# Cutting the last weight transfer of a decode kernel in two: the second half of the last wo block arrives as two transfers of one row each per partition

## The chip, the cores and the metric

The kernel runs on one core of one Trainium2 chip. The metric is device time in microseconds (us). "Before" is the kernel as it was, "the change" the kernel with the diff below.

The engines have their names from the profile: PE is the matrix engine (TensorE), DVE the vector engine, ACT the scalar engine, and SP (SyncE) here issues transfers and waits. A DMA transfer copies between the chip's main memory and its on-chip buffer. A semaphore is a counter on which an engine can wait; a transfer has "landed" when its semaphore has had all of its updates. The "chain of waits" is what the profile shows when it is followed back from the last instruction, at each step to what released it.

The unchanged kernel took 1344.42 us (median of 3 runs, 1344.25 to 1344.47). Its span in the profile, from the first to the last instruction, is 1342.8 us.

## The reference, cut to what matters

```python
# 4 sequences, one token each, model width 1024, 32 heads of 128, 8192 cached keys
q = (x @ wq) ...                                  # 4 x 32 heads x 128
p = softmax(q . k_cache * 128**-0.5)
o = p . v_cache
a = o.reshape(4, 32 * 128) @ wo                   # wo: 4096 x 1024, bf16, 8 MB
b = x + sigmoid(x . w_r) * ((silu(x @ w_gate) * (x @ w_up)) @ w_down)
out = sigmoid(x . gate_w) * a + (1 - sigmoid(x . gate_w)) * b     # 4 x 1 x 1024
```

The caches are 537 MB (512 MiB) of bf16 and the weights nearly all the rest of 576 MB. Every byte is read once, so the kernel is a long stream of loads. The product with wo comes last, because it needs the finished attention output.

## The kernel before

SP issues all loads in program order. wo is handled in 8 blocks, numbered 0 to 7. A block holds 512 rows of wo: four consecutive rows of 1024 elements for each of 128 partitions. One row is 2 KB of one partition, so a block is 8 KB per partition and 1 MB in all.

```python
FR = 4                      # rows of wo per partition and block
NB, NH = 512, 2             # a row is multiplied in two halves of 512 columns
wov = A_wo.rearrange("(g p r) n -> p g r n", p=P, r=FR)

def mm_acc(out_ap, lhsT, rhs, start=False):
    nc.tensor.matmul(out_ap, lhsT=lhsT, rhs=rhs, start=start, stop=True, skip_group_check=True)

def wo_block(g, r0=0, r1=FR):
    home, at = divmod(g, 4)
    # ... (a slot of the ring buffer holds four blocks)
    w = wo_home[home][:, at]
    nc.sync.dma_start(out=w[:, r0:r1].rearrange("p r n -> p (r n)"),
                      in_=wov[:, g, r0:r1].rearrange("p r n -> p (r n)"))
    def use():
        for r in range(r0, r1):
            for n in range(NH):
                mm_acc(acc[:, n * NB:(n + 1) * NB], LT[:, r, g, :], w[:, r, n * NB:(n + 1) * NB])
    return use

# ... the end of the kernel, NWB = 8:
last = [wo_block(g) for g in range(2, NWB - 2)]
last += [wo_block(g, r, r + FR // 2) for g in (NWB - 2, NWB - 1) for r in (0, FR // 2)]
last.pop(0)()
# ... (last of the attention output, flushed between the first blocks)
last.pop(0)()
o_rows(GE, NWB)
for use in last:
    use()
res = turned(Bn, D)
nc.vector.tensor_copy(out=res[:, 0:NB], in_=acc[:, 0:NB])
nc.sync.dma_start(out=out2[:, 0:NB], in_=res[:, 0:NB])
nc.scalar.copy(out=res[:, NB:D], in_=acc[:, NB:D])
nc.scalar.dma_start(out=out2[:, NB:D], in_=res[:, NB:D])
```

So blocks 2 to 5 come as one transfer of 1024 KB each, and blocks 6 and 7 as two of 512 KB each (two rows per partition). The wait for a transfer stands before the first matmul that reads it. DVE copies the first 512 output columns and ACT the second.

## Time and profile before

| | before |
|---|---|
| time, median of 3 runs | 1344.42 us |
| span in the profile | 1342.8 us |
| bytes moved, mean rate | 576.18 MB, 429 GB/s |
| PE / DVE busy | 77% / 46% |

The first extract is from the profile's page of the kernel before. The span is cut in 40 equal slices; each digit is the busy share of one slice in tenths, and the last row gives the rate in GB/s.

```profile
span 1342.8 us, 7621 instructions
PE   2665877787788687778987779598778679877897
DVE  2555655544346554335455546146555244556000
DMA  9999999999999999999999999999999999999997
GB/s 414 434 434 430 432 436 430 444 433 418 445 430 424 440 431 425 437 436 432 432 438 431 426 433 430 434 436 435 432 423 441 430 427 431 436 426 443 423 423 331
```

The DMA engines are busy from the first slice to the last, and only the last slice falls off. The kernel is bound by its stream. What is left to win is in the last slice, where the stream ends and something must still be done with what came last.

The second extract is the timeline of the last 6 us of the same kernel: start, duration, engine, line and operation; in brackets the idle time ahead of the instruction and what ended it. Weight loads (PEld) are left out.

```profile
1336.09 1.34 PE L279 MATMUL acc<-ring,LT 128*4 128x512 bf16 x5
...
1337.66 1.02 PE L279 MATMUL acc<-ring,LT 128*4 128x512 bf16 x4 [0.23 <-DMA ring<-in_A_wo_dram]
...
1338.89 1.02 PE L279 MATMUL acc<-ring,LT 128*4 128x512 bf16 x4 [0.21 <-DMA ring<-in_A_wo_dram]
...
1339.74 0.68 DVE L588 CAST TB<-acc 4x512 bf16<-4x512 f32 x1 [8.29 <-PE acc L279]
1339.95 0.57 ACT L590 CAST TB<-acc 4x512 bf16<-4x512 f32 x1 [13.55 <-PE acc L279]
1340.44 0.29 SPq L589 DMA_DIRECT2D out_dram<-TB  x1
1340.56 0.55 ACTq L591 DMA_DIRECT2D out_dram<-TB  x1
```

The third extract is the chain of waits that ended last, of the same kernel from 1325 us on: start, duration, what.

```profile
1323.81 15.04 DMA ring<-in_A_wo_dram
1338.85 0.04 issue
1338.89 1.04 PE acc L279 x4
1339.93 0.02 issue
1339.95 0.57 ACT TB L590
```

Read together: the last 512 KB land at 1338.85 us. Only then can four matmuls run, which end at 1339.93. ACT's copy follows, then the output transfer. PE waited 0.23 us and 0.21 us for the two last transfers.

Matmuls here start 0.216 us apart, and the last one takes 0.38 us to its modelled end. Four take 3 x 0.216 + 0.38 = 1.03 us.

The trace also records every DMA packet and every semaphore update. A transfer is shared among 16 engines, and each engine reports its own share, so the landing of a transfer has 16 times. For the last transfer of the kernel before they are these (us):

```
1332.23 1332.49 1332.68 1333.25 | 1336.70 1336.78 1336.83 1336.84 1337.03 1337.04 1337.18 1337.30 | 1338.23 1338.26 1338.66 1338.85
```

Four engines are done about 6 us before the last four. The transfer has landed when the slowest has its share. The last four 512 KB transfers landed at 1335.11, 1336.37, 1337.62 and 1338.85, one per 1.24 us. That is the slowest engine working off 8 packets of 4 KB at a time: the trace does not number the engines, but the packets that end with the last one can be followed back from 1338.27 us to 1332.20, each starting about 155 ns after the one before.

### The profile page before, as it was taken

How to read it: one execution, taken by the hardware profiler on the slowest of the kernel's cores; microseconds unless marked ns; L12 is line 12 of the kernel's file. 1: busy time of each engine (PE TensorE's matmuls, PEld its weight loads, DVE VectorE, ACT ScalarE, POOL GpSimd, SP SyncE). 2: the span in 40 equal slices, each digit the busy share in tenths (PEclk: the TensorE clock that was granted, in tenths of full speed). 3: DMA queues.
4: the chain of work that ended last, by engine and by line, in shares of the span. 5: the costliest groups of instructions: out<-in, count | busy, mean ns of one | idle time of the engine just before them, and what ended most of it. 6: DMA issues, size and time to landing. Idle time of an engine off the chain costs nothing.

```text
span 1342.8 us, 7621 instructions
## 1 busy us (share of the span) xinstructions
PE 1033.8 (77%) x4536; PEld 226.1 (17%) x2348; DVE 612.4 (46%) x358; ACT 50.6 (4%) x46; POOL 55.3 (4%) x90
## 2 busy tenths in 40 slices
PE   2665877787788687778987779598778679877897
PEld 0111111111111111111211112111111112111221
DVE  2555655544346554335455546146555244556000
ACT  0000100001000010001000010000100010000100
POOL 2000010001000010001000010000100010000100
PEclk9687988988999898889888889898889799889799
DMA  9999999999999999999999999999999999999997
GB/s 414 434 434 430 432 436 430 444 433 418 445 430 424 440 431 425 437 436 432 432 438 431 426 433 430 434 436 435 432 423 441 430 427 431 436 426 443 423 423 331
DMA packets 14172, 576.18 MB, mean 429 GB/s; under 512 B 1582, under 2 KB 1590, under 8 KB 2108
## 3 DMA queue, kind: packets, MB, share of 16 engines
q1 hardware_dynamic: 14132, 575.69, 99.5%
q8 instruction: 27, 0.44, 0.1%
q14 instruction: 5, 0.04, 0.0%
q10 hardware_dynamic: 8, 0.00, 0.0%
HBM read 575.68 MB, written 0.01 MB: 429 GB/s over the span
## 4 chain that ended last, share of the span: by engine, by line
DMA 65%; DVE 20%; PE 12%; another core or an unknown queue 1%; ACT 0%; issue 0%; SPq 0%; DVEq 0%
DMA ring<-in_A_k_cache_dram 56%; DVE TB L443 20%; PE o_ps L523 10%; DMA ring<-in_A_v_cache_dram 7%; DMA x<-in_gate_w_dram 2%; DMA ring<-in_A_wo_dram 1%; PE S_ps L449 1%; ACT PB L494 0%; PE S_ps L313 0%; PE acc L313 0%; PE small L543 0%; ACT OS L535 0%; PE acc L279 0%; DVE OS L536 0%
## 5 line engine op out<-in xcount | busy, mean ns | idle before, releaser
L443 DVE STREAM_TRANSPOSE TB<-ring 128x2048 uint32<-128x2048 uint32 x256 | 567.3, 2278 | 495.2 <-DMA ring<-in_A_k_cache_dram 493.9
L449 PE MATMUL S_ps<-TB,Z 128*128 128x512 bf16 x2048 | 520.0, 409 | 218.7 <-DVE TB L443 218.5
L523 PE MATMUL o_ps<-ring,PB 128*32 128x512 bf16 x2048 | 461.9, 389 | 52.5 <-DMA ring<-in_A_v_cache_dram 47.9
L449 PEld LDWEIGHTS <-Z 128*128 128x128 bf16 x1024 | 105.5, 103 | 628.8 <-issue 627.3
L523 PEld LDWEIGHTS <-PB 128*32 128x32 bf16 x1024 | 100.9, 99 | 410.0 <-issue 401.3
L536 DVE SCALAR_TENSOR_TENSOR OS<-o_ps,mE,OS 128x512 f32<-128x512 f32 x8 | 6.0, 751 | 104.1 <-ACT OS L535 104.1
L474 ACT ACTIVATE PTs<-S_ps,negm 128x1024 bf16<-128x1024 f32 x8 | 8.9, 1114 | 1024.9 <-DVE negm L471 1024.9
L425 POOL TENSOR_TENSOR Z<-qa,mq 128x16 bf16<-128x16 bf16 x32 | 9.1, 286 | 744.4 <-PE S_ps L449 654.7
L496 POOL COPY PB<-PT 32x1024 bf16<-32x1024 bf16 x16 | 30.4, 1903 | 82.1 <-PE o_ps L523 81.7
L494 ACT COPY PB<-PT 32x1024 bf16<-32x1024 bf16 x16 | 30.5, 1907 | 1.5 <-DVE PT L476 1.3
L376 DVE CAST LT<-small 128x64 bf16<-128x64 f32 x2 | 0.5, 225 | 40.6 <-PE small L374 40.6
L226 PE MATMUL small<-identb,x 6*128 6x6 bf16 x8 | 0.6, 197 | 22.6 <-DMA x<-in_gate_w_dram 22.6
L467 POOL PARTITION_ALL_REDUCE gmx<-mex x8 | 3.2, 396 | 340.7 <-DVE mex L464 340.7
L462 DVE TENSOR_REDUCE m<-S_ps 128x1 f32<-128x1024 f32 x8 | 9.8, 1225 | 15.9 <-PE S_ps L449 15.9
L279 PE MATMUL acc<-ring,LT 128*4 128x512 bf16 x64 | 15.0, 378 | 2.0 <-DMA ring<-in_A_wo_dram 1.4
L476 DVE STREAM_TRANSPOSE PT<-PTs 128x1024 bf16<-128x1024 bf16 x8 | 10.0, 1245 | 10.2 <-ACT PTs L474 10.2
L279 PE MATMUL acc<-ring,hT 128*4 128x512 bf16 x56 | 12.2, 379 | 0.0
L535 ACT ACTIVATE OS<-o_ps,mE 128x512 f32<-128x512 f32 x8 | 5.5, 687 | 158.8 <-PE o_ps L523 158.8
L313 PE MATMUL o_ps<-ring,xw 128*4 128x512 bf16 x56 | 6.0, 555 | 5.0 <-DMA ring<-in_B_w_gate_dram 5.0
L543 PEld LDWEIGHTS small<-selg,OS 128*128 128x128 f32 x64 | 9.0, 208 | 4.1 <-issue 3.9
L543 PE MATMUL small<-selg,OS 128*128 128x16 f32 x64 | 8.7, 269 | 0.0
L548 DVE SCALAR_TENSOR_TENSOR OT<-small,sgb,rinv 128x16 bf16<-128x16 f32 x8 | 1.8, 225 | 10.5 <-PE small L543 10.5
(71 smaller groups left out, 67.1 us busy)
## 6 DMA issues: line engine op xcount, KB each, us to landing
ring<-in_A_k_cache_dram SPq DMA_DIRECT2D x14, 4096.0 KB
ring<-in_A_v_cache_dram SPq DMA_DIRECT2D x14, 4096.0 KB, 31.2
ring<-in_B_w_gate_dram SPq DMA_DIRECT2D x1, 7168.0 KB, 37.6
ring<-in_B_w_up_dram SPq DMA_DIRECT2D x1, 7168.0 KB, 39.2
ring<-in_B_w_down_dram SPq DMA_DIRECT2D x2, 3584.0 KB, 27.5
ring<-in_A_wo_dram SPq DMA_DIRECT2D x6, 1024.0 KB, 21.0
ring<-in_A_v_cache_dram SPq DMA_DIRECT2D x2, 2048.0 KB, 26.8
ring<-in_A_v_cache_dram SPq DMA_DIRECT2D x4, 1024.0 KB, 25.0
```

What stands on the lines that cost most here:

```text
L279: nc.tensor.matmul(out_ap, lhsT=lhsT, rhs=rhs, start=start, stop=True, skip_group_check=True)
L313: nc.tensor.matmul(ps[32 * k:32 * k + Bn, z, :], lhsT=xT[TW * half + t], rhs=cols(w, t, 4 * z + k), start=(half + t == 0), stop=(half == 1 ...
L425: nc.gpsimd.tensor_tensor(out=Z[:, :, QP - 1:QP - 1 + P].rearrange("p e (q c) -> p e q c", c=QP)[:, :, :, 0], in0=qa[:, :, h0:h0 + NQ, b], ...
L443: nc.vector.transpose(out=flat_t.bitcast(U32), in_=kn[:, c * CJ * Dh:(c + 1) * CJ * Dh].bitcast(U32))
L449: nc.tensor.matmul(sps[:, z, :], lhsT=Z[:, he, s:s + P], rhs=T[:, 16 * z:16 * z + 16, half, :, e], start=(t == 0 and n == 0 and he == 0), ...
L462: nc.vector.tensor_reduce(out=m1[:], in_=sps[:].rearrange("p z n -> p (z n)"), axis=AX.X, op=ALU.max)
L474: nc.scalar.activation(out=PTs[:], in_=sps[:].rearrange("p z n -> p (z n)"), func=ACT.Exp, bias=negm[:, 0:1], scale=scale, accum_out=rs[:, ...
L476: nc.vector.transpose(out=PT[:].rearrange("p j i -> p (j i)"), in_=PTs[:])
L494: nc.scalar.copy(out=Bv[at, :, :, q, :], in_=Pv[at])
L496: nc.gpsimd.tensor_copy(out=Bv[at, :, :, q, :], in_=Pv[at])
L523: nc.tensor.matmul(o_ps[row:row + NM, e, :], lhsT=PB[:, RD * t + c, z, w].rearrange("p e s j -> p (e s j)"), rhs=vn[:, j0 * Dh:(j0 + 4) * ...
L543: nc.tensor.matmul(oT[:, :], lhsT=o_sb[:, q * Dh:(q + 1) * Dh], rhs=selg[:, q].rearrange("p t s -> p (t s)"), start=(q == 0), stop=(q == 3))
```

## The change

The intent: of the last 512 KB, the first row per partition can be multiplied while the second is still coming. So two matmuls instead of four are left when the last byte is there.

```diff
     last = [wo_block(g) for g in range(2, NWB - 2)]
-    last += [wo_block(g, r, r + FR // 2) for g in (NWB - 2, NWB - 1) for r in (0, FR // 2)]
+    cuts = [(NWB - 2, 0, 2), (NWB - 2, 2, 4), (NWB - 1, 0, 2), (NWB - 1, 2, 3), (NWB - 1, 3, 4)]
+    last += [wo_block(*cut) for cut in cuts]
     last.pop(0)()
```

Transfers, matmuls and their order stay otherwise as they were. SP issues one transfer more (two of 256 KB in place of one of 512 KB), and PE has one wait more, before the last two matmuls.

## The prediction

> **What bounds the kernel now.** The memory stream. The page of the kernel before shows a span of 1342.8 us, 429 GB/s on average and a DMA row at 9 tenths in 39 of 40 slices; PE is 77% busy, DVE 46%. The change touches only the last 5 us. There the chain of waits reads: landing of the last wo transfer until 1338.85 us, four matmuls 1338.89 to 1339.93 (1.04 us), the ACT copy at 1339.95 (0.57 us), then the output transfer. The timeline shows PE waiting 0.23 and 0.21 us for wo transfers before its last two groups of four matmuls.
>
> The packet records show what paces the end. The fastest engine's share of the last 512 KB transfer lands at 1332.23 us, the slowest's at 1338.85. On the slowest, the last four 512 KB transfers complete at 1335.11, 1336.37, 1337.62 and 1338.85, one per 1.24 us: 8 packets of 4 KB, 159 ns each. The last landing is that engine's backlog; the same bytes cannot land earlier.
>
> **What the change does.**
> - Bytes, matmuls and their order stay. The instruction order shows one more issue on SP and one more wait on PE, before the last two matmuls.
> - Removed from the chain: the two matmuls of row 2. Row 2 lands at about 1338.25 us, and its matmuls run while row 3 still comes. After the last landing two matmuls remain: one pitch of 0.216 us plus one duration of 0.38 us, 0.60 us instead of 1.04. Gain: 0.43 us.
> - Added: 2 KB packets in place of 4 KB ones. Packets of 16, 8 and 4 KB took 613, 313 and 159 ns, the few of 2 KB 84 ns; 16 x 84 instead of 8 x 159 ns would be 0.07 us on the slowest engine, rather less as starts are 155 ns apart. One semaphore packet (9 ns) comes on top. The Trainium skill, "DMA: Bandwidth & Descriptors", section "Why small descriptors are slow (HBM only)", names a fixed cost of about 3 cycles per packet, small at this size; the nearly proportional times agree. Cost: about 0.03 us, at most 0.08.
> - Moved: SP reuses 8 completion semaphores in turn, so the new last issue waits for a landing at 1326.24 us, not 1323.74. The fastest engine needs its packets only at about 1331, and an issue takes under 1 us to its first packet (the output: 1340.44 to 1341.20). Not critical; the extra 0.33 us on SP isn't either.
> - The latency after the last packet (0.43 us) is paid once at the end, as before.
>
> **Prediction.** 1344.42 - 0.43 + 0.03 = 1344.0 us; 8 in 10: 1343.6 to 1344.4. Faster by over 2%: 0.002; within 2%: 0.996; slower by over 2%: 0.002.
>
> **What would show each step.** The last landing comes as before, relative to the 512 KB landings ahead of it, within 0.1 us; another landing about 0.6 us before it; two matmuls in 0.60 us as the chain's last PE link; the ACT copy 0.4 us earlier; the tail after it (2.8 us) unchanged; 2 KB packets of 80 to 85 ns.
>
> **What would make it wrong.** Two-KB packets of over 100 ns, or a gap at each new transfer, would delay the last landing and eat the gain. A late last issue would matter only if the slowest engine starved too. The slowest engine's lag (6.6 us) may differ from run to run. The runs before spread over 0.22 us, half of the gain: its sign should be visible, its size barely.

## The result, and the profile after

Ratios here are the mean time of one kernel's runs over that of the other's of the same rounds, so not quite the ratio of the medians that are quoted.

| | before | the change |
|---|---|---|
| time, median of 6 runs | 1344.32 us (1344.12 to 1344.47) | 1343.95 us (1343.83 to 1344.16) |
| ratio | 1 | 0.9997 (95%: 0.9985 to 1.001) |
| span of the profiled run | 1342.8 us | 1342.2 us |

The medians differ by 0.37 us. The interval of the ratio includes 1, so this comparison alone does not prove a gain. Two repetitions below point the same way.

The page of the change has the same rows as before: the stream is busy to the end, with its drop in the last slice.

```profile
span 1342.2 us, 7623 instructions
DMA  9999999999999999999999999999999999999998
```

The timeline of the change, last 6 us, weight loads left out:

```profile
1335.96 3.48 PE L279 MATMUL acc<-ring,LT 128*4 128x512 bf16 x14
...
1339.26 0.68 DVE L589 CAST TB<-acc 4x512 bf16<-4x512 f32 x1 [7.72 <-PE acc L279]
1339.48 0.57 ACT L591 CAST TB<-acc 4x512 bf16<-4x512 f32 x1 [12.98 <-PE acc L279]
1339.97 0.29 SPq L590 DMA_DIRECT2D out_dram<-TB  x1
1340.08 0.54 ACTq L592 DMA_DIRECT2D out_dram<-TB  x1
```

Its chain of waits from 1325 us on:

```profile
1321.42 16.09 DMA ring<-in_A_wo_dram
1337.51 0.04 issue
1337.55 1.90 PE acc L279 x8
1339.45 0.02 issue
1339.48 0.57 ACT TB L591
```

Two things are to be seen. ACT's copy starts 0.47 us earlier; 0.10 us of it is that the stream came earlier in this trace (the fixed landing of the table below), and 0.38 us, about as predicted, is from the end itself. But the chain does not look as predicted. It does not run through the last landing and two matmuls. It runs through the third landing from the end (rows 0 and 1 of block 7, 1337.51 us) and all eight matmuls of the block, back to back. PE has no gap before its last matmuls.

The semaphore records say why. In the change, row 2 landed at 1338.16 us and row 3 at 1338.79. PE started row 0 at 1337.55 and could reach row 3 at 1337.55 + 6 x 0.216 = 1338.85 at the earliest. Row 3 was there for use at 1338.79 + 0.04 = 1338.83. Both limits meet within 0.02 us, and PE's own backlog (the matmuls that it still has to do before row 3) is the later one.

The waits of SP show the added issue. The columns are: who waited for whom, us in total, how often, the longest. The first extract is of the kernel before and the second of the change, both from 1320 us on.

```profile
SPq L386 <- DMA ring<-in_A_v_cache_dram: 4.2, 2, 2.1
SPq L617 <- DMA out_dram<-TB: 0.8, 1, 0.8
```

```profile
SPq L386 <- DMA ring<-in_A_v_cache_dram: 4.2, 2, 2.1
SPq L386 <- DMA ring<-in_A_wo_dram: 2.1, 1, 2.1
SPq L618 <- DMA out_dram<-TB: 0.8, 1, 0.8
```

The new last issue waits for a wo landing (1326.33 us in the change) before it may reuse that semaphore. The slowest engine needs the packets 11 us later.

### The profile page after: what moved, and what is told of

It reads as the page before. It is cut to its first block, busy times and chain, and to the rows that moved or that the text cites. A ratio compares the mean times of both kernels' runs of the same rounds, so it can differ in the third digit from the quotient of the medians.

```text
span 1342.2 us, 7623 instructions
## 1 busy us (share of the span) xinstructions
PE 1031.1 (77%) x4536; PEld 225.1 (17%) x2348; DVE 612.2 (46%) x358; ACT 50.6 (4%) x46; POOL 55.1 (4%) x90
## 4 chain that ended last, share of the span: by engine, by line
DMA 69%; DVE 19%; PE 10%; another core or an unknown queue 1%; issue 0%; ACT 0%; DVEq 0%; SPq 0%
DMA ring<-in_A_k_cache_dram 56%; DVE TB L443 19%; DMA ring<-in_A_v_cache_dram 10%; PE o_ps L523 7%; PE S_ps L449 2%; DMA x<-in_A_x_dram 2%; DMA ring<-in_A_wo_dram 1%; PE S_ps L313 0%; PE acc L313 0%; PE acc L279 0%; PE small L543 0%; DVE OS L536 0%; ACT OS L535 0%; PE small L226 0%
```

## The experiments

The stretch up to the last few transfers moves from one trace to the next by up to 0.6 us (see the first column below; e12, with other loads in the middle, apart). So I compare traces from one fixed event near the end: the landing of the second half of block 6, which is the same transfer, at the same place in the order, in every kernel. Everything below comes after it. The columns are: that landing; from it to the last landing; from it to the start of ACT's copy; from that start to the end of the span; from the landing to the end. All in us, from the trace records. By the run times every kernel here has, against the kernel before, an interval that includes 1, so the traces decide.

| kernel | landing | to last landing | to ACT's copy | copy to end | landing to end |
|---|---|---|---|---|---|
| before | 1336.37 | 2.48 | 3.59 | 2.82 | 6.40 |
| the change, first trace | 1336.27 | 2.53 | 3.21 | 2.76 | 5.97 |
| e1, the change again | 1336.26 | 2.53 | 3.21 | 2.77 | 5.97 |
| e9, the change, third time | 1336.51 | 2.52 | 3.20 | 2.76 | 5.96 |
| e2, split but used together | 1336.26 | 2.53 | 3.63 | 2.76 | 6.39 |
| e11, the same again | 1336.47 | 2.53 | 3.63 | 2.76 | 6.38 |
| e8, small pieces first | 1336.43 | 2.53 | 3.63 | 2.77 | 6.40 |
| e3, block 7 in one transfer | 1336.25 | 2.46 | 4.42 | 2.89 | 7.31 |
| e4, block 7 in four rows | 1336.20 | 2.57 | 3.24 | 2.86 | 6.10 |
| e5, row 3 in columns | 1335.94 | 2.56 | 3.22 | 2.86 | 6.07 |
| e6, rows and columns | 1335.99 | 2.62 | 3.07 | 2.90 | 5.97 |
| e10, the same again | 1336.29 | 2.60 | 3.06 | 2.92 | 5.98 |
| e7, eight half rows | 1336.01 | 2.69 | 3.15 | 2.91 | 6.06 |
| e12, as e6, other semaphores | 1337.11 | 2.60 | 3.07 | 2.77 | 5.84 |

Theory A: the gain is matmul work taken out from behind the last landing, less a small cost for smaller packets. Its two variants differ in what ends the changed kernel: the last landing (A1, as predicted) or PE's own eight matmuls (A2, as the chain shows). As the two limits met within 0.02 us, both may hold at once: then taking away only one of them gains nothing. Rival B: the gain comes from the transfers themselves (shorter ones, more of them, or the last one issued later).

### e1: the change again

No edit.

> The changed kernel once more, as the mark for the others of this set. Both theories: 0.37 us faster than the kernel before (the first comparison), with more runs. In its trace the eight matmuls of the last block run back to back from the third-last 512 KB-equivalent landing on, and end 1.90 us after they start.

Measured: 1343.84 us (1343.51 to 1343.97, 5 runs) against 1344.13 (1344.03 to 1344.37, 9 runs): 0.29 us, where 0.37 was expected. Here all five runs are below all nine. In the trace the eight matmuls again take 1.90 us without a gap, from 1337.54.

### e2: the split stays, but both rows are used behind the last landing

```diff
     last += [wo_block(*cut) for cut in cuts]
+    last[-2:] = last[:-3:-1]
```

PE multiplies row 3 first, so rows 3 and 2 both wait for row 3's landing. The transfers are those of the change.

> The two one-row transfers stay, in the same order, but row 3's matmuls are issued before row 2's, so that all four wait for the last landing. Theory A (the gain is matmul work taken out from behind the last landing): no gain left; 1.04 us of matmuls behind the last landing as before, plus the cost of the smaller packets, so 0.00 to 0.08 us slower than the kernel before. Rival B (the gain comes from the transfers themselves: shorter last transfer, later issue, earlier last landing): 0.37 us faster as the change.

Measured: 1344.36 us (1344.23 to 1344.90) against 1344.13. The gain is gone, and B with it. The chain of e2 ends as that of the kernel before did:

```profile
1338.79 0.04 issue
1338.83 1.04 PE acc L279 x4
```

The last landing is where e1 has it, 1338.79 us in both traces, and ACT's copy starts 0.42 us later than in e1. The median however lies 0.23 us above the kernel before, more than the 0.08 that I allowed; see e11.

### e3: block 7 in one transfer

```diff
-    cuts = [(NWB - 2, 0, 2), (NWB - 2, 2, 4), (NWB - 1, 0, 2), (NWB - 1, 2, 3), (NWB - 1, 3, 4)]
+    cuts = [(NWB - 2, 0, 2), (NWB - 2, 2, 4), (NWB - 1, 0, 4)]
```

> The last block comes as one transfer of 1024 KB, four rows per partition. Theory A: eight matmuls behind the last landing, 7 x 0.216 + 0.38 = 1.89 us instead of 1.04: 0.85 us slower than the kernel before (0.8 to 0.9), the landing itself within 0.05 us. Rival B gives no size; if smaller transfers as such cost, it should be faster.

Measured: 1345.27 us (1344.78 to 1345.66) against 1344.13: 1.14 us slower, more than the 0.8 to 0.9 expected. From the fixed landing to ACT's copy the trace shows 4.42 us, 0.83 more than before, which is the expected size; a further 0.07 us comes at the very end (2.89 against 2.82). The rest of the 1.14 is not seen in the last stretch of this one trace, so it stays unexplained. The chain shows the eight matmuls behind the last landing:

```profile
1338.70 0.04 issue
1338.75 1.90 PE acc L279 x8
```

### e5: row 3 in two halves of its columns

`wo_block` gets a column range, and row 3 is loaded and used as two pieces of 1 KB per partition.

```diff
-    cuts = [..., (NWB - 1, 0, 2), (NWB - 1, 2, 3), (NWB - 1, 3, 4)]
+    cuts = [..., (NWB - 1, 0, 2), (NWB - 1, 2, 3), (NWB - 1, 3, 4, 0, 1), (NWB - 1, 3, 4, 1, 2)]
```

> As the change, and row 3 comes as two transfers of half a row (1 KB per partition). Theory A1 (in the changed kernel the last landing still sets the end): one matmul behind it, 0.38 us in place of 0.60, less 0 to 0.08 for the packets: 0.14 to 0.22 us faster than the change. Theory A2 (in the changed kernel PE itself sets the end: its eight matmuls run back to back from the landing of rows 0 and 1): within 0.05 us of the change, the eight matmuls again 1.90 us without a gap, though the last landing leaves one matmul to go.

Measured: 1343.88 us (1343.72 to 1343.96), against 1343.84 of the change in the same set: nothing gained, as A2 says. The chain is again the landing of rows 0 and 1 and eight matmuls, although only one matmul depends on the last landing:

```profile
1337.19 0.04 issue
1337.23 1.90 PE acc L279 x8
```

From the fixed landing to ACT's copy it takes 3.22 us, as in the change (3.21). A1 expected 0.14 to 0.22 us less. The last landing came at 1338.50 us, but PE, already at work on the rows before, started its last matmul only at 1338.74.

### e6: rows 0 to 2 singly, row 3 in halves

With the column range of e5 in `wo_block`, as in e7, e10 and e12 too. Here and below, the line of the change that is replaced is left out, and "..." stands for the two pieces of block 6.

```diff
+    cuts = [..., (NWB - 1, 0, 1), (NWB - 1, 1, 2), (NWB - 1, 2, 3), (NWB - 1, 3, 4, 0, 1), (NWB - 1, 3, 4, 1, 2)]
```

> The last block's rows 0, 1 and 2 come as one transfer each, row 3 as two of half a row. Theory A2 (in the changed kernel PE's own eight matmuls set the end): with row 0 on hand a landing earlier PE has no backlog left, and one matmul (0.38 us) follows the last landing, which comes some 0.05 us later for the smaller packets: 0.10 to 0.20 us faster than the change (about 0.5 us faster than the kernel before). Theory A1 (the last landing set the end already) is not told apart by this run alone: 0.14 to 0.22 faster; it fell with the run before, where half rows alone gained nothing.

Measured: 1343.73 us (1343.54 to 1343.87) against 1344.17: 0.44 us faster than the kernel before. ACT's copy starts 3.07 us after the fixed landing, 0.14 less than in the change. e9 and e10, the same two kernels on one chip, show 0.15 (3.20 and 3.06). That is within the expectation: once PE is given row 0 earlier, the half rows pay. In e5 the same half rows without the earlier row 0 gained nothing, so PE's backlog held e5 back. In the chain PE's 24 matmuls of blocks 5 to 7 now stand in one piece:

```profile
1333.54 0.04 issue
1333.58 5.46 PE acc L279 x24
1339.04 0.02 issue
1339.07 0.57 ACT TB L594
```

By the semaphore records the last landing comes at 1338.61 us, and the one matmul that needs it starts at 1338.65. But from the fixed landing to the end e6 takes 5.97 us, as the change does. The 0.14 us were lost again after ACT's copy, which e12 explains.

### e4: block 7 in four rows

```diff
+    cuts = [..., *[(NWB - 1, r, r + 1) for r in range(4)]]
```

> The last block comes as four transfers of one row. Theory A2: takes the backlog off PE, but two matmuls then wait for the last landing as in the prediction, so 0.60 us behind it: the two limits lay within 0.03 us of each other, so within 0.05 us of the change. If PE's backlog were the only limit, it would be 0.2 us faster or more.

Measured: 1343.98 us (1343.82 to 1344.07) against 1344.17. ACT's copy comes after 3.24 us, 0.03 later than in the change, as expected. Here two matmuls stand behind the last landing, as the prediction had described it for the change:

```profile
1333.74 5.04 PE acc L279 x22
1338.78 0.04 issue
1338.81 0.61 PE acc L279 x2
```

The chain does not name the last landing, because the modelled end of the 22nd matmul (1338.78 us) falls together with it. The semaphore records have it at 1338.77, and the last two matmuls start 0.41 us after the one before, not 0.216. So PE waited for the landing. Without its backlog the kernel is no faster than the change, so the backlog was not the only limit there: e5 and e4 each take away one of the two limits and gain nothing, and e6, which takes away both, starts ACT's copy 0.14 us earlier.

### e7: block 7 in eight half rows

```diff
+    cuts = [..., *[(NWB - 1, r, r + 1, n, n + 1) for r in range(4) for n in range(2)]]
```

> The last block comes as eight transfers of half a row (1 KB per partition). One matmul (0.38 us) follows the last landing. Packets of 1 KB at 46 ns: by their starts a row in halves takes the slowest engine about 0.67 us instead of 0.62, four rows 0.15 us more than in the change: 0.05 to 0.12 us faster than the change. If the last issues, which now wait for a landing at about 1336.3 us, come too late for the slowest engine, or small packets cost by their durations (64 x 46 ns), it is 0.1 to 0.4 us slower than the change.

Measured: 1343.89 us (1343.78 to 1343.96) against 1344.17. The last landing comes 2.69 us after the fixed one, 0.16 later than in the change, where about 0.15 was expected. ACT's copy is 0.06 us earlier than in the change, within the expectation. The end is not: 6.06 us from the landing, 0.09 later than in the change, again for what follows ACT's copy. The last issues wait for landings near 1336 us and still arrive in time for the slowest engine.

### e8: the small pieces first

```diff
+    cuts = [..., (NWB - 1, 0, 1), (NWB - 1, 1, 2), (NWB - 1, 2, 4)]
```

> As many transfers and as many 2 KB packets as the change, but the one-row pieces are rows 0 and 1, and rows 2 and 3 come last, together. Theory A: four matmuls behind the last landing again, 1.04 us; 0.00 to 0.08 us slower than the kernel before, no gain. Rival B (more and smaller transfers, or the later last issue, bring the gain): 0.37 us faster than the kernel before.

Measured: 1344.07 us (1343.97 to 1344.58) against 1344.17: by medians 0.10 us faster, by means 0.04 us slower, so the run times do not tell. As many transfers, as many 2 KB packets and as late a last issue as in the change, and ACT's copy comes 3.63 us after the fixed landing, as in e2. Four matmuls stand behind the last landing again:

```profile
1338.96 0.04 issue
1339.00 1.04 PE acc L279 x4
```

B falls a second time.

### e9, e10, e11: the change, e6 and e2 again, on one chip

No new edits.

> The changed kernel again, beside the next two on one chip. 0.25 to 0.45 us faster than the kernel before; in the trace the ACT copy starts 3.21 us after the landing of the second half of the last but one block (kernel before 3.58).

> Rows 0 to 2 singly and row 3 in halves, again, directly against the change in one set. By the trace of the first run 0.13 us faster than the change (the ACT copy 3.08 us after the same landing). By the spread of runs so far (0.1 to 0.4 us within one set) the medians may show 0.0 to 0.25.

> The split with both rows used behind the last landing, again: its first median lay 0.23 us above the kernel before, where 0.00 to 0.08 was expected and its trace shows 0.05. If that excess was spread between runs: 0.0 to 0.15 us above the kernel before this time. If there is a cost that the end of the trace does not show: 0.2 us or more again.

Measured, against 1344.18 us (1344.09 to 1344.46) of the kernel before: the change 1343.97 (1343.78 to 1344.17), e6's tail 1343.86 (1343.69 to 1343.97), e2's tail 1344.26 (1344.08 to 1344.56). The change gained 0.21 us here, a little less than the 0.25 to 0.45 expected; its trace has the expected 3.20 us. e2's tail is now 0.08 us above the kernel before, so most of the 0.23 us of e2 was spread between runs. e6's tail is 0.11 us below the change with overlapping runs. Its trace from the landing to the end (5.98 against 5.96) shows no such gain, so I do not call it faster than the change.

### e12: e6 with the output's semaphores of the change

```diff
-        ks = load_pair(kv_view(A_k_cache, d), RING)
+        ks = load_pair(kv_view(A_k_cache, d), RING, apart=d in (8, 10, 13, 15, 18, 20))
```

Transfers take one of 8 completion semaphores in turn. At the end of the program SP checks all of them in a fixed order. In e6 and e10 the two output transfers have semaphores early in that order; in the change they have the last two. Six additional transfers in the middle of the program, together with e6's two, shift the turn by 8, which is once around.

> Rows 0 to 2 singly and row 3 in halves, and six K loads in the middle of the program split in two, so that the two output transfers get the same completion semaphores again as in the change (two fewer semaphores to check after them than without the six splits; SP checks all of them in a fixed order at the end, 65 ns apart). Theory C (the time from the ACT copy's start to the end depends on the output's place in that order): 2.76 us as in the change, not 2.90 to 2.92 as in the two runs of the same tail before; from the landing of the last but one block to the end 5.83 us, 0.13 us less than the change. Rival (the longer end comes with the smaller last transfers): 2.90 us again. The time of the whole, 0.5 us faster than the kernel before if the six splits cost nothing in the middle, which is not sure; so the verdict is read from the trace.

Measured: copy to end 2.77 us, as in the change, with the 3.07 us of e6 ahead of it. From the landing to the end it takes 5.84 us, the shortest of all, where 5.83 was expected. SP's records of the final checks (start in us; the last number of a pair names the DMA semaphore) show the difference. In the change the last two checks are those of the output:

```
the change: 1340.30 (104)  1340.37 (105)  1340.44 (108)  1341.25 (109, output)  1341.43 (110, output)  1341.49 next step
e6:         1339.87 (104)  1339.94 to 1340.99 (105, with 102: output)  1341.03 (108, with 101: output)  1341.10 (109)  1341.16 (110)  1341.22 next step
before:     1340.78 (104)  1340.85 (105)  1341.71 (108, output)  1341.89 (109, output)  1341.95 (110)  1342.02 next step
```

The checks that are still to do after the last landing of the output stand about 0.065 us apart. In the kernel before one is left, in the change none, in e6 three. The last but one column of the table follows their number: with none it is 2.76 to 2.77 us (the change, e2, e8, e11, e12), with one 2.82 (before), with two 2.86 to 2.89 (e3, e4, e5), with three 2.90 to 2.92 (e6, e7, e10). Adding one transfer moved the output's semaphores by one place, and that alone gave the change 0.06 us (2.82 against 2.76; e2 and e8, with as many transfers and no earlier matmuls, have 2.76 and 2.77 too).

The whole of e12 is not faster: 1344.45 us (1344.20 to 1344.66) against 1344.18. Its fixed landing comes at 1337.11 us, 0.60 to 0.85 us later than in the traces of the change. So the six splits in the middle seem to cost more than the end gained (one trace, and a median 0.27 us above the kernel before), and no kernel beats the change beyond doubt.

## Why the prediction was right, point by point

The predicted time was 1344.0 us, in a range of 1343.6 to 1344.4; 1343.95 was measured, and "within 2%" held. The gain was forecast at 0.40 us; the six runs of the comparison show 0.37. That this is so close is in part luck, as the points below say.

- **The gain of 0.43 us by two matmuls fewer behind the last landing.** Right in size. From the last landing to ACT's copy the kernel before takes 1.10 us and the change 0.69 (0.68 in e1 and e9): 0.41 to 0.42 us less. e2, e8 and e11 have the split and all four matmuls behind the last landing, and take 1.10 again. e3 puts eight there and takes 1.97.
- **"Two matmuls in 0.60 us as the chain's last PE link".** Wrong. The chain has eight matmuls in 1.90 us, released by the landing of rows 0 and 1. I had counted what depends on the last landing, but not whether PE would be free by then. Row 2's matmuls did not run while PE was idle; they ran behind a backlog that ended just as row 3 became usable. The two limits are 0.02 us apart, so the size came out right; for the prediction that was luck. Its own figures could have warned: PE needs 6 x 0.216 = 1.30 us from row 0 to row 3, and the last landing was to come 1.24 + 0.03 us after that of rows 0 and 1. e5 shows that PE's backlog is a limit even where the last landing leaves room, and e4 shows two matmuls behind the last landing once the backlog is gone, with no gain; in the change the two limits hold together.
- **The cost of smaller packets: 0.03 us, at most 0.08.** Measured 0.03 to 0.04 us (last landing 2.485 us after the fixed one before, 2.519 to 2.527 in the change). The 2 KB packets took 84 ns, within the 80 to 85 expected. On the slowest engine they start 80 ns apart and those of 4 KB about 155, so 16 in place of 8 take 16 x 80 - 8 x 155 = 40 ns more.
- **Later issue, not critical.** Right as far as tried: e2 and e8 have the same late issue and the end of the kernel before, and e7 issues far later still.
- **"The tail after it (2.8 us) unchanged".** Off by 0.06 us, for a reason I had not seen: the place of the output's semaphore in the final checks, shown by e12.
- **The sum.** From the fixed landing to the end the traces show 6.40 us before and 5.96 to 5.97 in the change, 0.43 to 0.44 less. The run times show 0.37, 0.29 and 0.21 us by medians in three sets. Why they show less than the trace is open. I have one trace of the kernel before, and its profiled run (1344.51 us) was slower than the medians of all its sets; the stretch ahead of the fixed landing moves by more than the missing 0.1 to 0.2 us.

The prediction cited the Trainium skill, "DMA: Bandwidth & Descriptors", section "Why small descriptors are slow (HBM only)", for a fixed cost of about 3 cycles per packet. If these are cycles of the 850 MHz fabric clock that the same page states, which is my assumption, the estimate is 3.5 ns. The runs agree in size: with block 7 in packets of 8 KB (e3), 2 KB (e4) and 1 KB (e7), the slowest engine has 8, 32 and 64 of them, and the last landing comes after 2.46, 2.57 and 2.69 us. That is 0.109 / 24 = 4.5 ns and 0.235 / 56 = 4.2 ns for each packet more, with the semaphore packets of three and seven additional transfers counted in.

## What to carry to other kernels

When a kernel ends on its last load, cut that load so that little work depends on the last piece, but then check that the engine doing the work is free when the piece lands. If it isn't, cut the piece before it too; in this kernel finer cuts of the last piece alone (e5) or of the piece before alone (e4) gained nothing, and only both together (e6) let the last copy start earlier. A control that keeps the split and takes away the early use (e2) tells a gain by overlap from a gain by the transfers at the cost of one edited line.

## What the Trainium skill lacked or had wrong

- "DMA: Bandwidth & Descriptors", section "Rules for kernel authors", advises at least 1 MiB per DMA for bandwidth and to coalesce small transfers. It does not separate a lone transfer from one in a full queue. Here, with the queue full, cutting 512 KB into two of 256 KB cost 0.04 us (2.485 to 2.527) and cutting 1 MB into eight of 128 KB cost 0.23 us (2.46 in e3 to 2.69 in e7), less than the overlap won.
- The same page, "Latency and other measured facts", says that two of the 16 engines (7 and 15) are usually slower. Here the engines end in three groups of 4, 8 and 4, over 6.6 us (1332.23 to 1338.85 in the kernel before). The page's best guess at a cause concerns transfers issued by GpSimd, and these are issued by SP. The trace does not number the engines, and no run here shows the cause. As the last landing waits for the slowest, this spread is far larger than the whole gain of the change.
- The same page, "Anatomy of one DMA — SWDGE (gpsimd) path", gives about 2 us of fixed cost, most of it after the last byte, for transfers issued by GpSimd. For transfers issued by SP, as here, I found no figure for the time after the last byte. The slowest engine's last data packet of the kernel before ended at 1338.43 us and its semaphore update came at 1338.85: 0.42 us.
- No page that I found says what the checks of the completion semaphores at the program's end cost: they stand about 0.065 us apart, and with none to three of them after the output's last landing it takes 2.76 to 2.92 us from the start of ACT's copy to the end (the change, e10) for the same work.
